# Attention scores listed ahead of older groups' work on TensorE, with six score tiles, eight tiles for maxima and two resident weight pairs fewer

## The chip, the core and the metric

The kernel runs on one core of a Trainium2 chip. The metric is the device time of one execution in microseconds (us). PE is TensorE, PEld its weight load, DVE is VectorE, ACT is ScalarE, POOL is GpSimd, and SP issues the transfers (DMA). Each engine runs its own list of instructions in the order of the program and waits on semaphores for the others.

## What is computed

```python
# q, k, v: 4 batches x 8 heads x 576 x 64, float32, tau = 0.02
scores = scale * q @ k.T
thresh = max(scores, axis=-1) - tau
scores = where(scores >= thresh, scores, -1e9)
attn = exp(scores - max(scores)); attn = attn / (sum(attn) + 1e-9)
x = (attn @ v)                      # as 2304 tokens x 512
h = x @ w_in;  x = (h * sigmoid(1.702 * h)) @ w_out          # d_ff 2048
h = x @ w_in2; out = (h * tanh(softplus(h))) @ w_out2
```

The weights of the two feed-forward layers come as 64-bit floats, and the kernel converts them on the chip.

## The kernel before

**Attention** works on 16 pairs of heads (a "head pair" below), each in five groups: four "full" groups of 128 query rows for both heads, and one "mix" group with the last 64 rows of both. That makes 80 groups, numbered 0 to 79. A group g goes through these steps:

- S(g), scores: `qk` (L600) has PE write the scores of both heads into the PSUM tiles `sc0` and `sc1`. There is one set of them, so S(g+1) must wait until both are read.
- DVE L622 reads a score tile, scales and negates it into an SBUF tile of the ring `ss` (four tiles, two per full group), and puts the negated maximum into a tile of the ring `nm`. POOL L626 adds tau to it.
- ACT L629 takes the exponential into a pair tile of the ring `p` (four, one per group). DVE L632 zeroes what lies below the threshold and sums the rows.
- T(g), transposes: PE L706 and L701 transpose the group's probabilities into `tb0`, `tb1`, `tb2`. ACT L717 copies them into `pm` and `pmt`.
- A(g), attention times v: PE L731 multiplies with `vr` into one half of the PSUM tile `tb3`, the two halves in turn. ACT L738 copies the result into `xo`.

After a head pair's fifth group, the sums are inverted (DVE L648, L649), spread over partitions through DRAM (`r_d`, `rb`), multiplied in (POOL L667) and stored.

**Layer 1** then loops over blocks of tokens and 16 slices f of d_ff: H(f), twelve matmuls into one of four banks `h` (L495), an activation on ACT and DVE (L521 to L527), and O(f), twelve matmuls into `tb0` to `tb3` (L540). PE's order is H0 H1 H2 O0 H3 O1 H4 O2 and so on. Layer 2 has the same shape.

**Weights.** Slice f needs a pair of tiles, `wh` and `wl`, in float32 parts. A chain makes them: a load into one of three `sr` tiles, ACT L380 and L382, DVE L386 and L389, POOL L392, DVE L394, ACT L400 (`wh`), DVE L402 (`wl`). In layer 1 the chain for slice f may start at group 40 + 5f. The first `NWA` pairs have memory from the start. The others lie where attention's tiles were, and wait until attention is over.

**What sets the order.** Nothing runs as it is written. Each piece of work is listed with an engine, a duration, the tiles that it reads and writes, and a rank. A planner (`Order.run`) steps through time: on each engine, of the pieces whose inputs and tiles are free, the one with the lowest rank goes next. The result is a fixed list for each engine. In attention the rank is the group's number, a little less for some steps: scores and transposes of group g have rank g on PE, and A(g) has g - 0.1. DVE's L622 has g - 2.5. The weights have ranks above 5000, so they go into what is left.

Of the kernel before, what the change touches and what calls it, by code (L numbers as in the profile page):

```python
# [11 lines left out]
F32 = mybir.dt.float32  # L12
# [7 lines left out]
SMR = 2.5  # L20
DMA_US = 2.0
DMA_RATE = 200e3
PR = 2
AR = 0.1
NORM_P = 1.0
# [7 lines left out]
SLACK = 0.0  # L33
AHEAD = 2
NP = 8
NSS = 4
NOUT = 2
NHS = 5
NWA = 12
NPM = 4  # L40
NKQ = 2
NXO = 2
# [8 lines left out]
class Order:  # L51
# [23 lines left out]
    def add(self, eng, dur, fn, r=(), w=(), rank=0.0, deps=(), nbytes=None, port=False, steps=1):  # L75
        n = len(self.ops)
        if port:
            self.port.add(n)
        before = set(deps)
        for key in r:  # L80
            if key in self.writer:
                before.add(self.writer[key])
        for key in w:
            if key in self.writer:
                before.add(self.writer[key])
            before.update(self.readers.get(key, ()))
        for key in r:
            self.readers.setdefault(key, []).append(n)
        for key in w:
            self.writer[key] = n  # L90
            self.readers[key] = []
        before.discard(n)
        self.ops.append((eng, dur, fn, before, rank, nbytes, steps))
        return n

    def run(self):
# [19 lines left out]
        while done < n_ops:  # L116
# [34 lines left out]
            if nbytes is not None:  # L151
                wire = end = max(wire, end + DMA_US) + nbytes / DMA_RATE
            order.append((t, i))
# [47 lines left out]
def attention_then_two_ffn_kernel(  # L201
# [46 lines left out]
    apool = att_ctx.enter_context(tc.tile_pool(name="a", bufs=1))  # L248
# [34 lines left out]
    tb = [psum.tile([128, 512], F32, name=f"tb{i}") for i in range(4)]  # L283
# [24 lines left out]
    def t_act(n, ptr=0, psum=True):  # L308
        return (0.05 if psum else 0.09) + n * 0.833e-3 + 0.093 * ptr
# [28 lines left out]
    def make_w(pool, upto):  # L338
        for f in range(len(W), upto):
            W.append([pool.tile([128, 2 * DM], F32R, name=f"w{p}{f}") for p in "hl"])  # L340

    make_w(wpool, NWA)

# [55 lines left out]
    def split_w(f, val, kval, rank):  # L399
        add("ACT", t_act(2 * DM, psum=False), lambda: nc.scalar.copy(W[f][0], val),  # L400
            [kval], [("wh", f)], rank, [opened] if f >= NWA else [])
        add("DVE", t_dve(2 * DM), lambda: nc.vector.tensor_tensor(W[f][1], val, W[f][0], ALU.subtract),  # L402
# [157 lines left out]
    vrs = Ring(apool, "vr", NKQ, [128, 5 * 128], F32)  # L560
    pps = Ring(apool, "p", NP // 2, [128, P1 + S + 1], F32)
    sss = Ring(apool, "ss", NSS, [128, S + 5], F32)
    nms = Ring(apool, "nm", 4, [128, 2], F32)
    sms = Ring(apool, "sm", 2, [128, 32], F32)
    rts = Ring(apool, "rt", 1, [128, 32], F32)
    rbs = Ring(apool, "rb", 1, [128, S], F32)
# [14 lines left out]
    def qk(tl, rank):  # L581

        kind, b, hp, t = tl
        kq2, _, kkq, _ = head[b, hp]
        q0 = S + t * 128

        def mm():
            if kind == "full":
                parts = [(i, sc[i][:, g, 0:SH], g * SH, SH) for g in range(2) for i in range(2)]
            else:  # L590
                lo, hi = sc[0][0:64], sc[0][64:128]
                parts = [
                    (0, lo[:, 0, 0:SH], 0, SH), (1, hi[:, 1, 0:512 - SH], SH + 64, 512 - SH),
                    (1, hi[:, 1, 512 - SH:SH], 0, 64),
                    (0, lo[:, 1, 0:SH], SH, SH), (1, hi[:, 0, 0:SH], 64, SH),
                ]
            for i, dst, k0, n in parts:
                rows = slice(64 * i, 64 * i + 64)
                q = kq2[rows, q0:q0 + (128 if kind == "full" else 64)]
                nc.tensor.matmul(dst, q, kq2[rows, k0:k0 + n], start=True, stop=True)  # L600
                yield

        n = 4 if kind == "full" else 2
        add("PE", n * 0.25 + 0.25, mm, [kkq], [("sc", i) for i in range(n)], rank,
            steps=4 if kind == "full" else 5)
        return [(sc[i][:, :, 0:SH], [("sc", 2 * i), ("sc", 2 * i + 1)]) for i in range(n // 2)]
# [68 lines left out]
    def attend(tl, ps, pair, rank):  # L675

        kind, b, hp, t = tl
        full = kind == "full"
        _, vr, _, kvr = head[b, hp]
        w = 128 if full else 64  # L680
        at = t * 128
        if t == 0:
            xo[b, hp] = xos.next()
        if full:
            plan = [(0, pms, (0, 1), 128, 512), (1, pms, (2, 3), 128, 512), (2, pmt, (4,), 128, 128)]
        else:
            plan = [(0, pms, (0, 1, 2, 3), 128, 512), (1, pmt, (4,), 64, 128)]
        where, copies, keys = {}, [], []
        for bank, ring, cs, rows, cols in plan:
            pn, kpn = ring.next()  # L690
            keys.append(kpn)
            for n, c in enumerate(cs):
                where[c] = (bank, n * 2 * w, pn)
            copies.append((bank, pn, kpn, rows, cols))

        def tr(cs):
            for c in cs:
                bank, c0, _ = where[c]
                if c == 4:
                    m = 64 * len(ps)  # L700
                    nc.tensor.transpose(tb[bank][0:m, 0:128], pair[:, 516:516 + m], ident)  # L701
                    yield
                    continue
                for i in range(len(ps)):
                    a = (P1 + 64 if i else 4) + c * 128
                    nc.tensor.transpose(  # L706
                        tb[bank][:, c0 + i * 128:c0 + (i + 1) * 128], pair[:, a:a + 128], ident)
                    yield

        for (bank, pn, kpn, rows, cols), (*_, cs, _, _) in zip(copies, plan):  # L710
            n = 1 if 4 in cs else len(ps) * len(cs)
            n = add("PE", n * 0.109 + (0.16 if bank == 0 else 0.0), lambda cs=cs: tr(cs),
                ps, [("tb", bank)], rank, steps=max(n, 2))
            if sch.fill is None and WARM:
                sch.fill = ("PE", n, 0.107, keep_warm)
            add("ACT", t_act(cols),
                lambda pn=pn, bank=bank, rows=rows, n=cols: nc.scalar.copy(pn[0:rows, 0:n], tb[bank][0:rows, 0:n]),  # L717
                [("tb", bank)], [kpn], rank)
        i = avn[0] % 2
        avn[0] += 1  # L720
        av, kav = tb[3][:, i * 128:i * 128 + w], ("tb", 3, i)

        def mm():
            for c in range(5):
                _, c0, pn = where[c]
                for i in range(2):
                    rows, at, vc = slice(0, 128), c0 + i * w, c * 128 + 64 * i
                    if c == 4:
                        rows = slice(64 * i, 64 * i + 64) if full else slice(0, 64)
                        at, vc = (0, 512) if full else (64 * i, 512 + 64 * i)  # L730
                    nc.tensor.matmul(  # L731
                        av[64 * i:64 * i + 64], vr[rows, vc:vc + 64], pn[rows, at:at + w],
                        start=(c == 0), stop=(c == 4))
                    yield

        add("PE", len(CK) * 0.107 * (2 if full else 1) + 0.2, mm, keys + [kvr], [kav], rank - AR, steps=2 * len(CK))
        x, kx = xo[b, hp]
        add("ACT", t_act(w), lambda: nc.scalar.copy(x[:, at:at + w], av), [kav], [kx + (t,)], rank - AR)  # L738
        if not full:
            scaling.append(scale_x(b, hp))  # L740

    avn = [0]
# [32 lines left out]
    for gi, tl in enumerate(groups + [None] * AHEAD):  # L775
        first = len(sch.ops)
        if tl:
            for bh in preps.get(gi, []):
                prep(*bh, gi - PR)
            kind, b, hp, t = tl  # L780
            if t == 0:
                sm[b, hp] = sms.next()
            sums, ksum = sm[b, hp]
            pair, kpair = pps.next()
            ps = [softmax_a(sums, ksum, 5 * i + t, gi, bank, (pair, kpair), i)
                  for i, bank in enumerate(qk(tl, gi))]
            marks.append(len(sch.ops) - 1)
            behind.append((tl, ps, pair, gi))
        if gi >= AHEAD:
            attend(*behind.pop(0))  # L790
            for todo in list(scaling):
                todo.pop()(gi - AR, [marks[min(gi, len(marks) - 1)]] if tl else [])
                if not todo:
                    scaling.remove(todo)
        if tl is None and gi == len(groups) + AHEAD - 1:
            for todo in scaling:
                while todo:
                    todo.pop()(gi - AR, [])
        att.extend(range(first, len(sch.ops)))
# [199 lines left out]
```

## Time and profile before

| what | value |
|---|---|
| median of 3 runs | 1096.7 us (1096.17 to 1097.32) |
| the profiled execution | 1097.12 us |
| its span, first to last instruction | 1095.3 us |
| PE busy | 1084.9 us (99%) |
| DVE busy | 692.8 us (63%) |
| ACT busy | 651.2 us (59%) |
| POOL busy | 196.4 us (18%) |
| mean granted clock of PE | 0.998 |

The profiled execution lies 1.8 us over its span and 0.4 us over the median. The busy shares are means over three stages that differ: attention up to about 312 us, layer 1 up to about 698 us, layer 2 to the end. A matmul's end is modelled in this profile, so that a busy PE can still be waiting for a part of its work. The distance from the start of one block of matmuls to the start of the next is the safer measure.

### The profile page before, as it was taken

The numbers are of one execution on the slowest core, as the hardware profiler recorded it, in microseconds if no ns is written. First come the engines' busy times: TensorE is split into PE (matmuls) and PEld (weight loads), VectorE is DVE, ScalarE is ACT, GpSimd is POOL, SyncE is SP. The second block draws the span as 40 slices with busy tenths as digits, with TensorE's granted clock in tenths as the row PEclk, the third lists the DMA queues.
The fourth block names the chain that finished last, engine by engine and source line by source line (L and its number), as shares of the span: only waits on it lengthen the run. The fifth ranks groups of instructions, "written<-read, shape, count | busy, mean of one in ns | idle before, by whom it ended". The sixth has DMA issues, their size and how long they took to land.

```text
span 1095.3 us, 17534 instructions
## 1 busy us (share of the span) xinstructions
PE 1084.9 (99%) x6708; PEld 877.5 (80%) x6708; DVE 692.8 (63%) x1354; ACT 651.2 (59%) x1065; POOL 196.4 (18%) x198
## 2 busy tenths in 40 slices
PE   9999999999999999999999999999999999999998
PEld 7767776777778899888888888888888888888887
DVE  7868899999978645545522444566464555554544
ACT  5767777888856445444422444496655655655665
POOL 2323344455534303303200000000000000000000
PEclk9999999999999999999999999999999999999999
DMA  2223333444244255545510222500010010010010
GB/s 90 82 76 125 92 118 127 146 128 149 95 161 140 94 202 173 199 148 184 181 58 1 97 96 96 173 1 1 29 39 1 10 39 1 1 40 1 1 40 19
DMA packets 49156, 94.53 MB, mean 86 GB/s; under 512 B 6320, under 2 KB 24240, under 8 KB 49072
## 3 DMA queue, kind: packets, MB, share of 16 engines
q1 hardware_dynamic: 49072, 93.42, 25.7%
q8 instruction: 52, 0.85, 0.3%
q14 instruction: 32, 0.26, 0.1%
HBM read 70.78 MB, written 22.62 MB: 85 GB/s over the span
## 4 chain that ended last, share of the span: by engine, by line
PE 97%; ACT 1%; DVE 1%; issue 0%; POOL 0%; POOLq 0%; DVEq 0%; ACTq 0%
PE h L495 36%; PE tb L540 18%; PE tb L911 18%; PE tb L731 9%; PE sc L600 8%; PE tb L706 7%; PE tb L701 1%; PE tb L506 0%; DVE p L632 0%; DVE ss L622 0%; ACT p L629 0%; POOL nm L626 0%; ACT pm L717 0%; ACT xo L738 0%; ACT sv L380 0%
## 5 line engine op out<-in xcount | busy, mean ns | idle before, releaser
L873 ACT ACTIVATE ms<-ms 128x512 f32<-128x512 f32 (+1 forms) x240 | 131.4, 584 | 133.5 <-DVE ms L858 132.5
L495 PE MATMUL h<-xa,wh 128*128 128x512 f32 x640 | 197.5, 390 | 0.0
L495 PE MATMUL h<-x,wh 128*128 128x512 f32 (+1 forms) x640 | 165.2, 346 | 0.0
L495 PEld LDWEIGHTS h<-xa,wh 128*128 128x128 f32 x640 | 119.7, 188 | 24.7 <-issue 0.2
L521 ACT ACTIVATE t<-h 128x512 f32<-128x512 f32 (+1 forms) x80 | 44.5, 557 | 155.3 <-PE h L495 154.7
L632 DVE SCALAR_TENSOR_TENSOR p<-ss,nm,p 128x577 f32<-128x577 f32 x144 | 130.0, 926 | 8.1 <-ACT p L629 6.4
L629 ACT ACTIVATE p<-ss,nm 128x576 f32<-128x576 f32 x144 | 111.5, 785 | 37.9 <-DVE ss L622 37.4
L524 DVE SCALAR_TENSOR_TENSOR h<-t,h 128x512 f32<-128x512 f32 (+1 forms) x80 | 51.3, 642 | 121.4 <-ACT t L521 121.2
L883 DVE TENSOR_TENSOR ms<-ms,hs 128x512 f32<-128x512 f32 (+1 forms) x80 | 50.2, 636 | 122.3 <-ACT ms L873 122.2
L622 DVE TENSOR_SCALAR_CACHE_REDUCE ss<-sc,nqsc 128x576 f32<-128x576 f32 x144 | 112.2, 812 | 21.1 <-PE sc L600 20.4
L495 PEld LDWEIGHTS h<-x,wh 128*128 128x128 f32 x640 | 112.7, 189 | 15.8
L495 PE MATMUL h<-xa,wl 128*128 128x512 f32 x320 | 124.5, 389 | 0.0
L626 POOL TENSOR_SCALAR nm<-nm,tau_p 128x1 f32<-128x1 f32 x144 | 88.0, 612 | 168.0 <-DVE ss L622 163.6
L540 PE MATMUL tb<-gh,wh 128*128 128x512 f32 (+1 forms) x320 | 117.8, 368 | 0.0
L540 PE MATMUL tb<-gl,wh 128*128 128x512 f32 (+1 forms) x320 | 117.7, 368 | 0.0
L540 PE MATMUL tb<-gh,wl 128*128 128x512 f32 (+1 forms) x320 | 117.7, 368 | 0.0
L392 POOL TENSOR_TENSOR sv<-sv,sr 128x1024 uint32<-128x1024 uint32 x32 | 83.4, 2608 | 175.7 <-DVE sv L389 104.8
L911 PE MATMUL tb<-wh,g2h 128*128 128x512 f32 x288 | 112.1, 389 | 0.0
L911 PE MATMUL tb<-wl,g2h 128*128 128x512 f32 x288 | 112.1, 389 | 0.0
L911 PE MATMUL tb<-wh,g2l 128*128 128x512 f32 x288 | 112.0, 389 | 0.0
L495 PE MATMUL h<-x,wl 128*128 128x512 f32 (+1 forms) x320 | 110.9, 347 | 0.0
L600 PE MATMUL sc<-kq 64*128 64x288 f32 (+3 forms) x672 | 105.0, 417 | 1.0 <-DVE ss L622 0.9
(59 smaller groups left out, 1756.0 us busy)
## 6 DMA issues: line engine op xcount, KB each, us to landing
sr<-in_w_in SPq DMA_DIRECT2D x32, 512.0 KB
sr<-in_w_out SPq DMA_DIRECT2D x32, 512.0 KB
kq<-in_kq SPq DMA_DIRECT2D x16, 576.0 KB
sv<-x_d SPq DMA_DIRECT2D x16, 512.0 KB
w_d<-sv SPq DMA_DIRECT2D x16, 512.0 KB
sv<-w_d SPq DMA_DIRECT2D x16, 512.0 KB
vr<-in_v SPq DMA_DIRECT2D x16, 320.0 KB
x_d<-xo SPq DMA_DIRECT2D x16, 288.0 KB
```

Of the source, the lines that this page charges most:

```text
L392: lambda: nc.gpsimd.tensor_tensor(bits, bits, word(0), ALU.add), keys, [kval], rank, port=True)
L495: nc.tensor.matmul(hb[dst][:, 0:n], a[:, c, :], x[:, lo, c, 0:n], start=(i == 0), stop=(i == 3 * KD - 1))
L540: nc.tensor.matmul(accs[e][0][:, 0:n], a[:, es], b()[:, 0:n], start=(f == 0 and i == 0), stop=(f == KF - 1 and i == 2), skip_group_check=True,
L600: nc.tensor.matmul(dst, q, kq2[rows, k0:k0 + n], start=True, stop=True)
L622: lambda: nc.vector.tensor_scalar(n3, s3, nqsc, None, ALU.mult, ALU.min, accum_out=nm[:, 0:1]),
L626: lambda: nc.gpsimd.tensor_scalar(nm[:, 1:2], nm[:, 0:1], tau_p, 0.0, ALU.add, ALU.add),
L629: lambda: nc.scalar.activation(p[:, at:at + S], ns[:, 4:4 + S], AF.Exp, bias=nm[:, 0:1], scale=-1.0),
L632: lambda: nc.vector.scalar_tensor_tensor(p[:, whole], ns[:, 3 + i:4 + S + i], nm[:, 1:2], p[:, whole], ALU.is_le, ALU.mult, accum_out=sums ...
L706: nc.tensor.transpose(tb[bank][:, c0 + i * 128:c0 + (i + 1) * 128], pair[:, a:a + 128], ident)
L731: nc.tensor.matmul(av[64 * i:64 * i + 64], vr[rows, vc:vc + 64], pn[rows, at:at + w], start=(c == 0), stop=(c == 4))
L873: nc.scalar.activation(m()[:, 0:n], m()[:, 0:n], fn, bias=bias)
L911: nc.tensor.matmul(accs[t][0], x[:, t * 128:(t + 1) * 128], w, start=(f == 0 and i == 0), stop=(f == KF - 1 and i == 2), skip_group_check= ...
```

## The change

Five things are edited. The scores' rank on PE becomes g - 8 instead of g, so that among ready work on PE the scores of a group come before transposes and products of groups up to seven older. The ring `ss` has six tiles instead of four, and `nm` eight instead of four. The product of a mix group goes into the unused half of `tb2` instead of a half of `tb3`. `NWA` falls from 12 to 10, so weight pairs 10 and 11 now wait for the end of attention too.

```diff
+SF = 8
...
-NSS = 4
+NSS = 6
...
-NWA = 12
+NWA = 10
...
-    nms = Ring(apool, "nm", 4, [128, 2], F32)
+    nms = Ring(apool, "nm", 8, [128, 2], F32)
...
-        i = avn[0] % 2
-        avn[0] += 1
-        av, kav = tb[3][:, i * 128:i * 128 + w], ("tb", 3, i)
+        if full:
+            i = avn[0] % 2
+            avn[0] += 1
+            av, kav = tb[3][:, i * 128:i * 128 + w], ("tb", 3, i)
+        else:
+            av, kav = tb[2][:, 256:256 + w], ("tb", 2, 1)
...
-                  for i, bank in enumerate(qk(tl, gi))]
+                  for i, bank in enumerate(qk(tl, gi - SF))]
```

Line numbers after the edits are one to four higher than before. The planner's lists show what moves. In its rows a name ends in a tile's number within the program; `p0` to `p3` are the pair tiles of groups 4n to 4n+3.

First place: PE around group 14, the mix group of the third head pair. Before, from T(14) on (L706 and L701 are transposes, L731 products, L600 scores):

```order
L706 MATMUL tb0_91<-ident_100,p2_158 128x128 x4
L701 MATMUL tb1_92<-ident_100,p2_158 64x128
L731 MATMUL tb3_94<-pm0_172,vr0_154 64x128 x4
L731 MATMUL tb3_94<-pm1_173,vr0_154 64x128 x4
L731 MATMUL tb3_94<-pmt1_177,vr0_154 64x128 x2
L731 MATMUL tb3_94<-pm2_174,vr0_154 64x64 x8
L731 MATMUL tb3_94<-pmt0_176,vr0_154 64x64 x2
L600 MATMUL sc0_98<-kq1_153 128x288
L600 MATMUL sc1_99<-kq1_153 128x288
L600 MATMUL sc0_98<-kq1_153 128x288
L600 MATMUL sc1_99<-kq1_153 128x288
```

These are T(14), A(13), A(14) and then S(15): no score stood between S(14) and S(15) while the transposes of groups 12 to 14 and the products A(11) to A(14) went by. Now, from A(13) on:

```order
L735 MATMUL tb3_94<-pm0_174,vr0_150 64x128 x4
L735 MATMUL tb3_94<-pm1_175,vr0_150 64x128 x4
L735 MATMUL tb3_94<-pmt1_179,vr0_150 64x128 x2
L702 MATMUL tb1_92<-ident_100,p2_154 64x128
L707 MATMUL tb0_91<-ident_100,p3_155 128x128 x4
L601 MATMUL sc0_98<-kq1_149 128x288
L601 MATMUL sc1_99<-kq1_149 128x288
L601 MATMUL sc0_98<-kq1_149 128x288
L601 MATMUL sc1_99<-kq1_149 128x288
L735 MATMUL tb2_93<-pm2_176,vr0_150 64x64 x8
L735 MATMUL tb2_93<-pmt0_178,vr0_150 64x64 x2
L707 MATMUL tb1_92<-ident_100,p3_155 128x128 x4
```

Here S(18) stands between A(13) and A(14), and A(14) writes `tb2`. Over the whole list, the last scores ahead of a product A(g) are now S(g+5) in 46 of the 75 cases up to H0 and S(g+4) in 18; before they were S(g+3) in 65 of 77. Changes from one kind of work to another, from S(0) to O0, fall from 252 to 243, since the transposes stand in 84 blocks instead of 93.

Second place: PE from the last score matmuls, S(79), to the first of layer 1, H0. Before:

```order
L600 MATMUL sc0_98<-kq1_153 64x288 x2
L706 MATMUL tb0_91<-ident_100,p1_157 128x128 x4
L731 MATMUL tb3_94<-pm1_173,vr1_155 64x128 x4
L731 MATMUL tb3_94<-pm2_174,vr1_155 64x128 x4
L731 MATMUL tb3_94<-pmt0_176,vr1_155 64x128 x2
L706 MATMUL tb1_92<-ident_100,p1_157 128x128 x4
L701 MATMUL tb2_93<-ident_100,p1_157 128x128
L706 MATMUL tb0_91<-ident_100,p2_158 128x128 x4
L495 MATMUL h0_3113<-xa_151,wh0_116 128x512 x2
```

Now:

```order
L601 MATMUL sc0_98<-kq1_149 64x288 x2
L707 MATMUL tb0_91<-ident_100,p2_154 128x128 x4
L702 MATMUL tb1_92<-ident_100,p2_154 64x128
L702 MATMUL tb2_93<-ident_100,p3_155 128x128
L707 MATMUL tb0_91<-ident_100,p3_155 128x128 x4
L735 MATMUL tb2_93<-pm2_176,vr0_150 64x64 x8
L735 MATMUL tb2_93<-pmt0_178,vr0_150 64x64 x2
L707 MATMUL tb1_92<-ident_100,p3_155 128x128 x4
L707 MATMUL tb0_91<-ident_100,p0_152 128x128 x4
L702 MATMUL tb2_93<-ident_100,p0_152 128x128
L496 MATMUL h0_3061<-xa_147,wh0_116 128x512 x2
```

H0 moves ahead by two groups' work: before, A(77) to A(79) and the transposes T(78) in part and T(79) stand behind H0; now A(75) to A(79) and T(76) in part to T(79) do. Before O0 stand, in both, all of attention and H0, H1, H2. The last pieces before O0 are, before, A(78) H2 T(79) A(79), and now H2 A(77) T(78) T(79) A(78) T(79) A(79).

Third place: DVE from the last L622, that of group 79, on (L402 makes `wl`, L394 the step of the weights' chain ahead of `wh`, L524 and L527 belong to layer 1). Before:

```order
L622 TENSOR_SCALAR ss3_163,nm3_167<-sc0_98,nqsc_103 128x576
L632 SCALAR_TENSOR_TENSOR p2_158,sm1_169<-ss2_162,nm2_166,p2_158 128x577
L402 TENSOR_TENSOR wl4_125<-sv0_113,wh4_124 128x1024
L394 SCALAR_TENSOR_TENSOR sv1_114<-sr2_112,sv1_114 128x1024
L386 TENSOR_SCALAR sv2_115<-sv2_115 128x1024
L386 TENSOR_SCALAR sv0_113<-sv0_113 128x1024
L389 TENSOR_SCALAR sv2_115<-sv2_115 128x1024
L402 TENSOR_TENSOR wl5_127<-sv1_114,wh5_126 128x1024
L389 TENSOR_SCALAR sv0_113<-sv0_113 128x1024
L524 SCALAR_TENSOR_TENSOR h0_3113<-t0_143,h0_3113 128x512
```

Now:

```order
L623 TENSOR_SCALAR ss5_161,nm7_169<-sc0_98,nqsc_103 128x576
L633 SCALAR_TENSOR_TENSOR p1_153,sm1_171<-ss1_157,nm3_165,p1_153 128x577
L633 SCALAR_TENSOR_TENSOR p1_153,sm1_171<-ss2_158,nm4_166,p1_153 128x577
L633 SCALAR_TENSOR_TENSOR p2_154,sm1_171<-ss3_159,nm5_167,p2_154 128x577
L633 SCALAR_TENSOR_TENSOR p2_154,sm1_171<-ss4_160,nm6_168,p2_154 128x577
L395 SCALAR_TENSOR_TENSOR sv2_115<-sr0_110,sv2_115 128x1024
L395 SCALAR_TENSOR_TENSOR sv0_113<-sr1_111,sv0_113 128x1024
L390 TENSOR_SCALAR sv1_114<-sv1_114 128x1024
L525 SCALAR_TENSOR_TENSOR h0_3061<-t0_139,h0_3061 128x512
L528 TENSOR_TENSOR gl0_144<-h0_3061,gh0_141 128x512
L633 SCALAR_TENSOR_TENSOR p3_155,sm1_171<-ss5_161,nm7_169,p3_155 128x577
```

Before layer 1's first L524, six weight pairs were finished (`wl0` to `wl5`); now three are (`wl0` to `wl2`), and `wl3`, `wl4`, `wl5` follow behind the L524 of slices 1 and 2. The last threshold step of attention (L632 of group 79) stood behind L527 of slice 1 and now stands behind that of slice 0. From `wl8` on, both lists put the pairs at about the same place among layer 1's steps.

## Rows read from the trace of the kernel before

**Rows 1.** Timeline of PE, attention at full pace: start us, us, instruction, [idle before].

```profile
284.17 0.66 PE L706 MATMUL tb<-ident,p 128*128 128x128 f32 x4
...
284.87 1.24 PE L600 MATMUL sc<-kq 64*128 64x288 f32 x8
286.44 0.69 PE L731 MATMUL tb<-pm,vr 128*64 128x64 f32 x16 [0.33 <-ACT pm L717]
...
287.32 1.09 PE L706 MATMUL tb<-ident,p 128*128 128x128 f32 x8
...
288.45 1.24 PE L600 MATMUL sc<-kq 64*128 64x288 f32 x8
289.62 1.09 PE L731 MATMUL tb<-pm,vr 128*64 128x128 f32 x16
...
291.01 1.09 PE L706 MATMUL tb<-ident,p 128*128 128x128 f32 x8
...
292.15 1.20 PE L600 MATMUL sc<-kq 64*64 64x288 f32 x10
293.27 0.65 PE L706 MATMUL tb<-ident,p 128*128 128x128 f32 x4
```

**Rows 2.** Timeline of PE: the first scores, and the first O block.

```profile
5.80 1.24 PE L600 MATMUL sc<-kq 64*128 64x288 f32 x8
...
311.87 0.50 PE L540 MATMUL tb<-gh,wh 128*128 128x512 f32 x1
```

**Rows 3.** Groups of PE, 12 to 312 us: count, busy, mean ns, idle before, its releasers.

```profile
L600 PE MATMUL sc<-kq 64*128 64x288 f32 (+3 forms) x655 | 102.2, 417 | 1.0 <-DVE ss L622 0.9
L706 PE MATMUL tb<-ident,p 128*128 128x128 f32 x568 | 83.5, 282 | 1.5 <-DVE p L632 1.5
L731 PE MATMUL tb<-pm,vr 128*64 128x128 f32 (+1 forms) x1280 | 82.0, 269 | 2.7 <-ACT pm L717 1.4 <-ACT xo L738 1.1
```

**Rows 4.** Timeline of PE and one row of DVE, where scores came late.

```profile
63.30 0.82 DVE L622 TENSOR_SCALAR_CACHE_REDUCE ss<-sc,nqsc 128x576 f32<-128x576 f32 x1 [5.63 <-PE sc L600]
...
64.18 1.97 PE L600 MATMUL sc<-kq 64*128 64x288 f32 x8 [0.91 <-DVE ss L622]
...
66.85 1.51 PE L706 MATMUL tb<-ident,p 128*128 128x128 f32 x7 [0.44 <-DVE p L632]
```

**Rows 5.** Windows: stretch, us, busy of PE, PEld, DVE, ACT, POOL, granted clock, DMA.

```profile
66.00:68.00 2.00, 1.56 (x9) 1.29 (x9) 2.00 (x5) 0.43 (x1) 0.29 (x1) 0.79 0.00 0
68.00:70.00 2.00, 2.00 (x9) 1.35 (x9) 1.10 (x4) 2.00 (x5) 0.90 (x1) 0.50 0.01 4
...
175.00:300.00 125.00, 124.30 (x1248) 89.35 (x1248) 121.74 (x280) 105.75 (x210) 63.75 (x74) 1.00 0.41 132
300.00:375.00 75.00, 73.18 (x362) 59.63 (x359) 61.83 (x71) 44.88 (x63) 32.40 (x11) 1.00 0.41 137
```

**Rows 6.** Timeline of PE at attention's last two blocks.

```profile
309.14 0.66 PE L706 MATMUL tb<-ident,p 128*128 128x128 f32 x4 [0.73 <-DVE p L632]
...
310.99 0.69 PE L731 MATMUL tb<-pm,vr 128*64 128x64 f32 x16 [1.09 <-ACT pm L717]
```

**Rows 7.** Timeline of DVE and PE: the weight pairs 14 and 15, and H(14) and H(15).

```profile
370.54 1.22 DVE L402 TENSOR_TENSOR wl<-sv,wh 128x1024 fp32r<-128x1024 f32 x1
...
374.01 1.23 DVE L402 TENSOR_TENSOR wl<-sv,wh 128x1024 fp32r<-128x1024 f32 x1 [0.51 <-ACT wh L400]
...
374.56 0.62 PE L495 MATMUL h<-xa,wh 128*128 128x512 f32 x2
...
380.00 0.62 PE L495 MATMUL h<-xa,wh 128*128 128x512 f32 x2
```

**Rows 8.** Line L394 of DVE, one per weight pair, 290 to 376 us: ns min/median/max, first and last start.

```profile
L394 DVE SCALAR_TENSOR_TENSOR sv<-sr,sv x11: 1162/1214/1226, 296.2 to 371.7; 128x1024 uint32<-128x1024 uint32 x11
```

**Rows 9.** Timeline of SP: the last store of attention's result.

```profile
330.25 0.33 SPq L669 DMA_DIRECT2D x_d<-xo  x1
```

## Prediction

> **What bounds the kernel now.** First the table: PE is busy 99% of the span, at full clock but for a dip. From O0 on it runs twelve matmuls every 2.72 us (H(14) and the O block behind it take 5.44 us, [rows 7]) and is without idle time, so layers 1 and 2 hold no time to win; they can only lose, if a weight pair comes late. What the change can win lies between the first scores at 5.80 and O0 at 311.87, 306.07 us [rows 2].
>
> How much of that is work? In the timeline of PE at full pace, start to start, a full group takes 1.17 for S (288.45 to 289.62), 1.39 for A (to 291.01) and 1.14 for T (to 292.15): 3.70 us. A mix group takes 1.12 (292.15 to 293.27), 0.88 (286.44 to 287.32) and 0.70 (284.17 to 284.87): 2.70 [rows 1]. So 64 x 3.70 + 16 x 2.70 = 280.0; H0 to H2 add 8.2, and sixteen warm-up transposes between S(0) and S(1) about 2.0 (an estimate at 1.14 / 9 each). That is 290.2, and 15.9 us are something else:
>
> - Idle PE: 1.0 + 1.5 + 2.7 = 5.2 by what ended it [rows 3]. It sits in two bad places and some small ones. At 64 to 67 us PE waits 0.91 and 0.44 [rows 4]: the list had let products and transposes of four groups go ahead of S(15), DVE had stood 5.63 us without a score, and PE then waited for DVE to catch up. At 309 to 312 us it waits 0.73 and 1.09 for attention's last group [rows 6]. That is 1.35 + 1.82 = 3.17 in the two, 2.0 elsewhere.
> - The clock: behind the first bad place the mean grant is 0.79 and then 0.50 over two stretches of 2 us, that is, PE fell to the lower of its two levels, 1.2 GHz, for a part of them, right after the waits at 64 to 67 us [rows 4, 5]. Lost: 0.21 x 2 + 0.50 x 2 = 1.4.
> - Split transposes: 9 in one block take 1.14, 5 take 0.70, so one costs 0.11 and a block's end 0.15. They stand in 93 blocks where 80 would do: 13 x 0.15 = 2.0.
> - The rest, 7.3, is hidden in blocks that look busy. An example is S at 284.87, which takes 1.57 instead of 1.17 [rows 1], as when its second tile is still being read by DVE.
>
> **The change, part by part.**
>
> *Scores first.* No instruction of PE is added. The bad place at 64 us goes: in the new list S(15) to S(18) stand ahead of A(14), DVE has scores to work on, and its 1.35 us go, with the dip behind it, 1.4. Nothing like the stretch without a score is left in the list. The last group's chain goes too: S(79) is now followed by the work of groups 74 to 78 and H0 to H2 before T(79), and the last L632 stands behind L527 of slice 0 instead of slice 1 (third place in the list). That is 1.82. Elsewhere I take the new list to be as tight as the old one outside its bad places, 2.0 idle and 7.3 hidden, neither better nor worse; the bounds are none of the 7.3 left, and as much again. Nine blocks of transposes fewer give 9 x 0.15 = 1.4 (1.35).
>
> *More tiles for scaled scores and maxima.* They let L622 go three groups ahead of L632 instead of two; without them the lead of S could not grow. They cost four one-column clears on DVE before the first score, which PE's warm-up covers.
>
> *Products of mix groups in `tb2`.* Idle time that ends with ACT's copy of `xo` is 1.1 us in all [rows 3]. I count none of it, because the halves of `tb3` still alternate for full groups; all of it is the upper bound.
>
> *Two weight pairs without memory of their own, and all pairs later.* Here a loss can come from. At layer 1's first L524, three pairs are ready instead of six. Today pair 14 is finished at 370.54 + 1.22 = 371.76 for H(14) at 374.56, and pair 15 at 375.24 for H(15) at 380.00: a slack of 2.8 and 4.8 us [rows 7]. Pairs come 7.55 us apart there ((371.7 - 296.2) / 10, [rows 8]), but slices are needed every 5.44, so the chain as it runs now loses ground. What hides the added work is DVE's idle time: from 300 to 375 us it is busy 61.83 of 75, 13.2 free [rows 5]. Three more pairs need about 3 x 3.8 = 11.4 (two steps of 1.22 each, two that I take at 0.7). It just fits. Also, H0 starts about two groups' T and A, 2 x 2.53 = 5.1 us, earlier in PE's list, and DVE steps of the chain that stand behind L524 follow it. Pairs 10 and 11 wait for attention's last store, issued at 330.25, 18.4 us behind O0 [rows 9]; H(10) starts 2.72 + 7 x 5.44 = 40.8 us behind O0, so that wait costs nothing unless `wh` is made more than 20 us ahead. I take no stall. The bounds are 0 and one pair behind, 7.55 - 2.8 = 4.8.
>
> Sum: 3.17 + 1.42 + 1.35 = 5.9 us. The profiled execution of 1097.1 becomes 1091.2, and since it lay 0.4 over the median, I say 1090.8, a gain of 0.54%. About 0.2%, or 2.2 us, is what a measurement of this kernel can tell from no change.
>
> **The rivals.**
>
> *The weights cap the gain.* If the pairs come at the times of today, H(14) cannot start before 371.8 and H(15) not before 375.2, whatever attention gains: the gain is 2.8 to 4.8 us, so 1091.9 to 1093.9. For it: the chain is slower than its use [rows 8]. Against: its steps on DVE stand behind layer 1's, which come earlier.
>
> *The weights come late: slower.* Place: PE waits at H(12) to H(15). If they are d us later than today, the whole is d - 2.8 slower; from d = 5.0 on it is slower by 0.2%. One pair's distance, 7.55, gives 4.8 us: 1101.5. For it: three pairs fewer at the start, and DVE would have to be busy 73.2 of 75. Against: part of DVE's idle time was waiting for layer 1.
>
> *Scores just in time.* A score that is listed the moment its tiles should come free blocks PE if DVE is late, with ready transposes queued behind it. The row for it is the S that took 0.40 too long [rows 1]. If fifteen more scores of the 80 are held so, 6.0 us are gone and the result is today's, about 1096.5; from twenty it is slower than today by 2.1. For it: in 175 to 300 us DVE is busy 121.74 of 125 [rows 5]. Against: DVE has three pairs' work, 11.4 us, less in attention. The Trainium skill (TensorE: Matmul & The Clock Gate, The mechanism) speaks for it: matmuls start and end strictly in program order, and only weight loads are pulled ahead. The trace agrees: at 66.85 and 309.14 PE stood still with other matmuls queued [rows 4, 6]. By that rule alone every late score is paid in full.
>
> *The lead does nothing.* The ring `p` still has four pair tiles, so exponentials of group g wait for T(g-4). If DVE is the bound from 175 us on, scores ahead only wait longer, and the repaired tail alone is left: 1.8 us, 1094.9, no change that can be told.
>
> **How the numbers follow.** Forecast (gain of 4.5 us or more) 0.52; capped by the weights 0.14; just in time 0.16; no effect 0.07; late weights 0.11. Faster: 0.52 + 0.12 of the cap's 0.14 = 0.64. Same: 0.02 of the cap, 0.12 of just in time, 0.07 = 0.21. Slower: 0.11 + 0.04 = 0.15. For the range: if half of the 7.3 hidden and all 1.1 of `xo` go too, it is 4.7 lower, 1086.1; I start at 1086.5. Above, it takes in the cap, no change, and late weights up to d = 5.1: 1099.0.
>
> **What would show it.** The step on scores is right if the timeline of PE has no idle time over 0.4 us before H0, a clock of 1.00 from 50 to 75 us, and O0 at about 306. The step on weights is right if PE has no idle time from O0 to H(16), with pair 15 finished before H(15). The forecast is wrong if PE's idle time before scores, or S blocks longer than 1.17, add up to more than now, or if H(12) to H(15) wait for L402.

## The result, and the profile after

| | before | after |
|---|---|---|
| median | 1096.97 us (1096.17 to 1097.32, 4 runs) | 1088.44 us (1088.21 to 1088.53, 4 runs) |
| profiled execution | 1097.12 us | 1088.53 us |
| its span | 1095.3 us | 1086.8 us |
| S(0) to O0 | 306.07 us | 297.55 us |

The ratio is 0.9918 (0.9906 to 0.9931): 8.5 us, or 0.8%, faster. O0 comes at 303.33 instead of 311.87. From there to the end both kernels take 783.4 us, so the whole gain lies before O0, in attention.

First, the groups of PE from 12 to 304 us (count, busy, mean ns, idle before, its releasers), to be held against [rows 3].

```profile
L601 PE MATMUL sc<-kq 64*128 64x288 f32 (+3 forms) x655 | 98.8, 413 | 1.0 <-DVE ss L623 1.0
L707 PE MATMUL tb<-ident,p 128*128 128x128 f32 x568 | 82.1, 278 | 1.6 <-ACT pm L718 1.6
L735 PE MATMUL tb<-pm,vr 128*64 128x128 f32 (+1 forms) x1280 | 81.0, 269 | 0.0
L735 PE MATMUL tb<-pmt,vr 64*64 64x128 f32 (+1 forms) x320 | 33.2, 284 | 0.4 <-ACT pmt L718 0.4
L702 PE MATMUL tb<-ident,p 128*128 128x128 f32 (+1 forms) x79 | 22.7, 290 | 0.2 <-ACT pm L718 0.2
```

Idle time fell from 5.2 to 3.2 us. Its kind changed too: the waits for `xo` and for L632 (L633 now) are gone, and 2.2 us of waits for the copies into `pm` and `pmt` are there.

Where the first bad place was [rows 4], PE's timeline now has a score between any two products, at the pace of [rows 1]: 1.17 from S to A, 61.04 to 62.21.

```profile
61.04 1.24 PE L601 MATMUL sc<-kq 64*128 64x288 f32 x8
62.21 1.09 PE L735 MATMUL tb<-pm,vr 128*64 128x128 f32 x16
...
64.27 1.24 PE L601 MATMUL sc<-kq 64*128 64x288 f32 x8
65.44 0.69 PE L735 MATMUL tb<-pm,vr 128*64 128x64 f32 x16
...
67.01 1.20 PE L601 MATMUL sc<-kq 64*64 64x288 f32 x10
```

The windows (columns as in [rows 5]) show the full clock there. In 300 to 375 us PE has 1.4 us more work than before in the same stretch, with DVE as busy as before.

```profile
66.00:70.00 4.00, 4.00 (x49) 2.81 (x43) 3.60 (x11) 3.37 (x7) 1.74 (x3) 1.00 0.46 120
70.00:75.00 5.00, 4.81 (x48) 3.42 (x46) 4.16 (x11) 3.32 (x9) 2.00 (x3) 1.00 0.40 147
175.00:300.00 125.00, 123.44 (x1244) 90.59 (x1239) 118.69 (x270) 101.41 (x206) 55.45 (x67) 1.00 0.40 125
300.00:375.00 75.00, 74.60 (x362) 61.45 (x360) 61.87 (x67) 46.24 (x62) 31.95 (x11) 1.00 0.43 141
```

The end of attention on PE, where 0.73 and 1.09 stood [rows 6], has one wait of 0.40.

```profile
301.99 0.69 PE L735 MATMUL tb<-pm,vr 128*64 128x64 f32 x16
303.07 0.33 PE L735 MATMUL tb<-pmt,vr 64*64 64x64 f32 x4 [0.40 <-ACT pmt L718]
303.33 0.50 PE L541 MATMUL tb<-gh,wh 128*128 128x512 f32 x1
```

The weight pairs 14 and 15 on DVE, and H(14) and H(15) on PE, as in [rows 7]: pair 15 is ready at 371.21 for an H(15) at 371.47. The slack of 4.8 us has become 0.3 (the first matmul that reads that `wl` starts at 371.93), and PE still does not wait.

```profile
361.71 1.22 DVE L403 TENSOR_TENSOR wl<-sv,wh 128x1024 fp32r<-128x1024 f32 x1
...
366.03 0.62 PE L496 MATMUL h<-xa,wh 128*128 128x512 f32 x2
...
369.98 1.23 DVE L403 TENSOR_TENSOR wl<-sv,wh 128x1024 fp32r<-128x1024 f32 x1 [1.12 <-ACT wh L401]
...
371.47 0.62 PE L496 MATMUL h<-xa,wh 128*128 128x512 f32 x2
```

**Where the 8.5 us came from.** Take PE's timeline from S(0) to O0, block by block, from one start to the next, and subtract from each block the idle time that the trace shows in it:

| | before | after | difference |
|---|---|---|---|
| S blocks | 99.6 | 96.0 | -3.6 |
| T blocks | 86.4 | 85.2 | -1.3 |
| A blocks | 104.1 | 102.4 | -1.6 |
| H blocks and warm-up | 10.8 | 10.7 | -0.1 |
| idle | 5.2 | 3.25 | -2.0 |
| sum | 306.1 | 297.55 | -8.5 |

The clock sits in the first two rows. Experiment 3 gives its share: there both bad places are still as they were, idle is 5.18, but the clock did not fall in that execution, and the S and T blocks are 0.8 and 0.6 us shorter: 1.4 together. Its A blocks are 0.5 shorter for another reason. Two products in a row, of a full and a mix group, took 2.59 and 2.49 net of idle in the kernel before (at 59.08 and 119.38) and take 2.27 with `tb2`. Experiment 4, which lacks `tb2` and has the full clock at both places, still shows 2.59 and 2.49. So this 0.5 is the work of `tb2`, not of the clock. Net of the clock, 2.8 (S), 0.65 (T) and 1.6 (A) went: 5.1 us that looked like busy PE.

On DVE, the waits of L622 for scores before 300 us fell from 17.1 us to 5.8. First before, then after (total, times, longest):

```profile
DVE ss L622 <- PE sc L600: 17.1, 23, 5.6
```

```profile
DVE ss L623 <- PE sc L601: 5.8, 16, 0.7
```

### The profile page after: what moved, and what is told of

It is laid out like the page before. It is cut to its first block, busy times and chain, and to the rows that moved or that the text cites. A ratio compares the mean times of both kernels' runs of the same rounds, so it can differ in the third digit from the quotient of the medians.

```text
span 1086.8 us, 17469 instructions
## 1 busy us (share of the span) xinstructions
PE 1078.3 (99%) x6708; PEld 873.7 (80%) x6708; DVE 690.9 (64%) x1358; ACT 651.3 (60%) x1065; POOL 184.0 (17%) x198
## 4 chain that ended last, share of the span: by engine, by line
PE 98%; ACT 1%; DVE 1%; issue 0%; POOL 0%; ACTq 0%; DVEq 0%; POOLq 0%
PE h L496 36%; PE tb L541 18%; PE tb L915 18%; PE tb L735 9%; PE sc L601 8%; PE tb L707 6%; PE tb L702 1%; ACT pm L718 1%; DVE p L633 0%; PE tb L507 0%; DVE ss L623 0%; ACT p L630 0%; DVE o L927 0%; DVE sv L387 0%; ACT gh L527 0%
## 5 line engine op out<-in xcount | busy, mean ns | idle before, releaser
L633 DVE SCALAR_TENSOR_TENSOR p<-ss,nm,p 128x577 f32<-128x577 f32 x144 | 130.8, 932 | 15.7 <-ACT p L630 8.3
L623 DVE TENSOR_SCALAR_CACHE_REDUCE ss<-sc,nqsc 128x576 f32<-128x576 f32 x144 | 112.2, 812 | 9.7 <-PE sc L601 9.0
L627 POOL TENSOR_SCALAR nm<-nm,tau_p 128x1 f32<-128x1 f32 x144 | 75.1, 522 | 167.5 <-DVE ss L623 165.1
```

Source lines behind the costliest of these rows:

```text
L623: lambda: nc.vector.tensor_scalar(n3, s3, nqsc, None, ALU.mult, ALU.min, accum_out=nm[:, 0:1]),
L627: lambda: nc.gpsimd.tensor_scalar(nm[:, 1:2], nm[:, 0:1], tau_p, 0.0, ALU.add, ALU.add),
L633: lambda: nc.vector.scalar_tensor_tensor(p[:, whole], ns[:, 3 + i:4 + S + i], nm[:, 1:2], p[:, whole], ALU.is_le, ALU.mult, accum_out=sums ...
```

## The experiments

The theory: the new order of scores is the whole gain, since it leaves no stretch in which DVE has no score; the tiles, `tb2` and `NWA` only allow it. Rivals: the extra tiles, or `tb2`, win time by themselves; fewer resident pairs cost some of it; scores that are merely earlier anywhere are enough. Unless another base is named, an edit is made to the kernel before, and the ratio is to before, with its 95% interval.

**1. All tiles, `tb2` and `NWA`, scores back at rank g** (base: after).

```diff
-SF = 8
+SF = 0
```

> The changed kernel with the scores' rank back at g (SF = 0): six score tiles, eight tiles for maxima, ten resident pairs and the product in tb2 stay. In its list the lead of S over A is 3 again in 58 of 76 cases, and four products still pass without a score around group 14. Theory 'the order is it': the place at 64 us comes back with its clock dip, the tail may be mended, so 1094 to 1096.5. Rival 'the tiles are it': the room for scaled scores carries the gain, and it stays at 1088 to 1090.

1095.26 us, ratio 0.9987 (0.9978 to 0.9996). O0 is at 310.82, and the waits of 0.91 and 0.5 us at 63 to 66 us are back. Without the rank the other edits are worth 0.1%.

**2. The rank and `tb2` alone**: four `ss`, four `nm`, twelve pairs.

```diff
-        i = avn[0] % 2
-        avn[0] += 1
-        av, kav = tb[3][:, i * 128:i * 128 + w], ("tb", 3, i)
+        if full:
+            i = avn[0] % 2
+            avn[0] += 1
+            av, kav = tb[3][:, i * 128:i * 128 + w], ("tb", 3, i)
+        else:
+            av, kav = tb[2][:, 256:256 + w], ("tb", 2, 1)
...
-                  for i, bank in enumerate(qk(tl, gi))]
+                  for i, bank in enumerate(qk(tl, gi - 8))]
```

> The kernel before with the rank g - 8 and the product in tb2 alone: four score tiles, four tiles for maxima, twelve resident pairs. The lead of S over A is 4 or 5 in 65 cases, 84 blocks of transposes, five pairs ready at H0 instead of three. Theory 'the order is it': O0 at 303 to 305 us, 1088.5 to 1090.5. Rival 'the tiles are it': scores wait for L622, L622 waits for a free score tile, S blocks stretch to more than before, 1093 to 1097.

1088.16 us (1087.53 to 1088.52), ratio 0.9919 (0.9905 to 0.9932): all of the gain. O0 is at 302.74. Pair 14 is ready 1.0 us before H(14), and pair 15 2.4 us before H(15) (368.37 and 370.74). So the extra tiles add nothing that can be measured, and with twelve pairs the slack is small too. The lead did grow with four tiles: the last score ahead of A(g) is S(g+4) or S(g+5) in 65 of 76 cases. The rank with the mix product left in `tb3` wasn't tried, since two products would then write one bank side by side without an order between them; that `tb2` makes the rank possible is all that is claimed for it.

**3. `tb2` alone** (the first hunk of experiment 2).

> The kernel before with the product of mix groups in tb2 and nothing else; the list is that of before. The idle time of PE that ends with the copy to xo was 1.1 us. If it was that half of tb3, PE's idle time there goes and the time falls by 0.5 to 1.1 us, to 1095.8 to 1096.4; by the prediction, which counted nothing, 1096.9.

1096.78 us, ratio 0.9996 (0.9987 to 1.0005): nothing that the ratio can tell. In the trace, two of the three waits for `xo` give way to waits of 0.34 us for `pmt`, and the A blocks lose the 0.5 us named above. The profiled execution kept its clock behind the same gaps: in its window the grant is 1.00, where a mean of 0.79 and 0.50 stood [rows 5].

```profile
66.00:70.00 4.00, 3.96 (x36) 2.90 (x36) 3.83 (x11) 3.24 (x6) 1.49 (x3) 1.00 0.01 2
```

**4. Two resident pairs fewer, alone.**

```diff
-NWA = 12
+NWA = 10
```

> The kernel before with ten resident weight pairs instead of twelve; the list up to H0 is that of before. Theory 'no cost': wh of slice 10 was written at 340 us, 10 us behind the last store of attention, so nothing waits: 1096.5 to 1097.3. Rival 'late pairs': the two pairs wait for attention's memory, the chain behind them is late, and H(12) to H(15) wait: 1098.5 to 1102.

1097.49 us, ratio 1.0003 (0.9994 to 1.0012), every pair with its slack of before or up to 1.5 us more. No cost.

**5, 6 and 7. The rank in one part of the program**: `tb2`, and g - 8 for groups 0 to 23, 24 to 69, or 70 to 79.

```diff
+                  for i, bank in enumerate(qk(tl, gi - (8 if gi < 24 else 0)))]
```

> The kernel before with the product in tb2 and the rank g - 8 for groups 0 to 23 alone. In its list the stretch around group 14 without a score is gone, the tail is nearly as before. By the prediction's terms: 0.91 + 0.44 of idle time and up to 1.4 of clock, 1.4 to 2.8 us, so 1094.3 to 1095.8. Rival 'only the lead everywhere counts': within 0.5 us of before.

> The kernel before with the product in tb2 and the rank g - 8 for groups 24 to 69 alone. The bad place at 64 us stays. By the prediction, which took the hidden 7.3 us and the small idle times as unchanged, only the tail changes (T(79) two blocks later): 1095 to 1097. Rival 'the hidden waits in S blocks go too': S blocks sum to about 97 us instead of 100.8 before O0, and the time falls by 3 to 5 us, to 1092 to 1094.

> The kernel before with the product in tb2 and the rank g - 8 for groups 70 to 79 alone. By the prediction the tail's 0.73 + 1.09 = 1.8 us go: 1095.2. Rival 'the tail only moves': the last chain waits elsewhere, 1096.5 to 1097.

Groups 0 to 23: 1094.56 us, ratio 0.9979 (0.9970 to 0.9988). The bad place at 64 us is gone. The two waits at the end of attention are gone as well, though no rank was changed there: the planner's list shifts behind an edit too. But the waits of 64 us, the same to the hundredth of a microsecond, stand further on in PE's timeline:

```profile
151.68 1.97 PE L600 MATMUL sc<-kq 64*128 64x288 f32 x8 [0.91 <-DVE ss L622]
...
154.35 0.98 PE L706 MATMUL tb<-ident,p 128*128 128x128 f32 x7 [0.44 <-DVE p L632]
```

Groups 24 to 69: 1098.35 us, ratio 1.0010 (1.0001 to 1.0019). In that trace the place at 64 us is as before, and three scores further on wait 0.76, 0.92 and 1.24 us for L622. Groups 70 to 79: 1101.63 us, ratio 1.0041 (1.0028 to 1.0053), slower. This is the rival "scores just in time", and the forecast of a gain for experiment 7 fell. In its trace the end of attention has one wait of 1.59 us instead of two of 1.8 in sum. PE's waits from 255 to 300 us are four for L622, and one of 0.2 us for `pm`; the S blocks are 2.6 us longer than in experiment 3, net of idle. In 265 to 283 us DVE is busy without a break while PE is not:

```profile
PE sc L600 <- DVE ss L622: 2.4, 4, 0.7
```

```profile
265.00:283.00 18.00, 15.83 (x145) 10.48 (x141) 18.00 (x42) 14.19 (x28) 12.95 (x12) 1.00 0.36 112
```

Each time, the products and transposes listed behind the score stood too. The Trainium skill (TensorE: Matmul & The Clock Gate, The mechanism) says that matmuls start and end in program order; these four waits agree with it. Scores early in one part only are therefore not enough.

**8 and 10. A lead of three.** Experiment 8 is after with SF = 3. Experiment 10 is before with `tb2` and g - 3, so with four `ss`, four `nm`, twelve pairs.

```diff
-                  for i, bank in enumerate(qk(tl, gi))]
+                  for i, bank in enumerate(qk(tl, gi - 3))]
```

> The changed kernel with SF = 3 instead of 8. In its list the lead of S over A is 3 in 71 of 76 cases, as before the change, but no more than two products pass between scores; transposes stand in 108 blocks instead of 84; six pairs are ready at H0. If a block's end costs 0.15 us, as the prediction says, 24 more blocks cost 3.6 us and the time is about 1092. Rival 'the block ends are free', since the transposes now wait for copies anyway: 1088 to 1089.5. Rival 'the lead of five groups is needed': scores wait as before, 1094 or more.

> The kernel before with the product in tb2 and the rank g - 3: four score tiles, twelve pairs, a lead of 3 in 73 of 77 cases, 109 blocks of transposes, six pairs at H0. Theory 'an even order is it, the lead and the tiles are not': 1089 to 1091, with pair 15 ready 8 us or more ahead of H(15). Rival 'the even order needs the six tiles': scores wait, 1093 or more.

1090.12 us, ratio 0.9939 (0.9926 to 0.9951), and 1089.29 us, ratio 0.9934 (0.9921 to 0.9946). In both lists the last score ahead of a product is S(g+3) almost throughout, as before the change. So 7 to 8 of the 8.5 us need no longer lead. What differs from before is the order: at most two products stand between two scores, where four did at S(15). That count is not all of it, since the list of experiment 9 below keeps to it too and gains less. From the start of one group's score to the next, the longest stretch on PE is 9.8 us before, 6.3 in experiment 9, and 4.8 in experiments 8 and 10; in the changed kernel it is 4.9. The two waits at the end of attention are one of 0.62 in experiment 8 and none in experiment 10. The waits of PE in experiment 10, 12 to 310 us, are down to one:

```profile
PE sc L600 <- DVE ss L622: 0.2, 1, 0.2
```

These lists split the transposes into 108 and 109 blocks instead of 84. T then takes 88.05 us net of idle instead of 85.15 in both, 2.9 for 24 or 25 blocks: 0.12 each.

**9. Only the stretch without scores mended**: `tb2` and g - 1. The list is nearly that of before, its lead and the two waits at its end too (0.71 and 1.11 us here), but no more than two products stand between scores.

```diff
-                  for i, bank in enumerate(qk(tl, gi))]
+                  for i, bank in enumerate(qk(tl, gi - 1))]
```

> The kernel before with the product in tb2 and the rank g - 1. Its list is nearly that of before: a lead of 3 in 65 of 77 cases, 94 blocks of transposes, the same tail, six pairs at H0, but no more than two products pass between scores. Theory 'the stretch without scores is a cause of its own': DVE's 5 us wait for scores at 63 us goes, with the 1.35 us behind it and the dip, so 1094 to 1095.5, and the tail's 1.8 us stay. Rival 'order matters only through the lead': 1096 to 1097.5.

1093.61 us, ratio 0.9972 (0.9961 to 0.9984), 3.2 us under experiment 3. But its six executions fall into two groups by the granted clock: three at 1.00 take 1092.6 to 1092.7 us, three at 0.998 take 1094.5 to 1094.8. Like against like, it is 2.3 to 2.4 us under experiment 3 (1094.98 at 1.00, a median of 1096.97 at 0.998). So the stretch is a cause of its own, of that size, and the clock still falls in half of the executions without it.

**11. The weights' chain started later** (base: after).

```diff
-C0 = 40
+C0 = 60
```

> The changed kernel with the weights' chain of slice f allowed from group 60 + 5f instead of 40 + 5f; two pairs instead of three are ready at H0. Theory 'the weights cap the gain': pair 15 is ready 0.3 us ahead of H(15) in the changed kernel, so one pair fewer at H0 (a pair is 7 us of its chain) shows as idle time of PE that ends with L403 among H(3) to H(15), 3 to 10 us, and the time is 1091 to 1098. Rival 'the chain has room': DVE and ACT have idle time enough to catch up, no idle time of PE, 1088 to 1089.

1092.94 us, ratio 0.9966 (0.9953 to 0.9979), 4.5 us over after. Attention is even shorter, O0 at 302.22, but layer 1 now waits for weights. PE, then DVE (one period of the chain):

```profile
359.81 0.50 PE L496 MATMUL h<-xa,wl 128*128 128x512 f32 x1 [0.53 <-DVE wl L403]
...
366.14 0.50 PE L496 MATMUL h<-xa,wl 128*128 128x512 f32 x1 [0.53 <-DVE wl L403]
```

```profile
358.53 1.22 DVE L403 TENSOR_TENSOR wl<-sv,wh 128x1024 fp32r<-128x1024 f32 x1
359.67 0.68 DVE L528 TENSOR_TENSOR gl<-h,gh 128x512 fp32r<-128x512 f32 x1
360.27 2.33 DVE L387 TENSOR_SCALAR sv<-sv 128x1024 f32<-128x1024 f32 x1
362.52 1.21 DVE L395 SCALAR_TENSOR_TENSOR sv<-sr,sv 128x1024 uint32<-128x1024 uint32 x1
363.66 0.68 DVE L525 SCALAR_TENSOR_TENSOR h<-t,h 128x512 f32<-128x512 f32 x1
364.26 0.68 DVE L390 TENSOR_SCALAR sv<-sv 128x1024 uint32<-128x1024 uint32 x1
364.86 1.22 DVE L403 TENSOR_TENSOR wl<-sv,wh 128x1024 fp32r<-128x1024 f32 x1
```

DVE has no gap, and a pair comes every 6.33 us (358.53 to 364.86) where PE could use one every 5.44. Not all of that is work: L387 takes 2.33 here and 0.69 in the median, and ends 0.55 behind a step of POOL that takes 358.74 to 362.05 (the last section says more). L395 needs the result of that POOL step, so no run shows how much shorter the period could be. The rival "the weights cap the gain" is a real limit, and with 0.3 us of slack the changed kernel stands right before it.

**12. Experiment 7 without weights in its way**: the same rank, and the chain only from group 78 on.

```diff
-C0 = 40
+C0 = 78
```

> The run with the rank g - 8 for groups 70 to 79 alone, and the weights' chain allowed only from group 78 on. Layer 1 then waits long for its weights, so the whole time says nothing (1130 or more); what counts is PE before H0. Theory 'DVE, loaded with weight pairs, makes the early scores late': the four waits of S for L622 at 266 to 286 us, 2.4 us in all, are gone. Rival 'the sudden lead does it': they stay, 1.5 us or more.

One execution, 1127.51 us, since layer 1 then waits for weights (PE is idle for 12.9 us from O0 on). Only attention is read. PE's waits from 255 to 300 us, and the window of experiment 7:

```profile
PE tb L706 <- ACT pm L717: 0.6, 3, 0.2
```

```profile
265.00:283.00 18.00, 17.82 (x183) 12.98 (x183) 16.55 (x41) 12.99 (x30) 7.48 (x13) 1.00 0.22 70
```

No score waits for L622 any more. So the four waits of experiment 7 hang on the weights' chain. Its steps on DVE (L386, L389, L394, L402) are busy 13.1 us in 255 to 300 us there, and not at all here. The edit also takes away the chain's steps on ACT and POOL, and the planner makes another list without them, so which of these made the scores late is not separated; that it was DVE's load is argued. Nor does a run show why the rank in every group escapes such waits with the chain in place. Before group 70, where both keep rank g, the waits of 0.91 and 0.44 us appear here at 64, 192 and 248 us although no weight step runs. Those are a matter of the list alone.

## Why the prediction was nearly right

The direction, the place and the mechanism of the bad places were right, and the time lies in the range; but the range, 1086.5 to 1099.0, held no change at all as well. The gain was taken too small: 5.9 us against 8.6 in the profiled execution. That it came so near is in part luck. The three terms of the sum, 5.9, measure 4.0 (2.0 idle, 1.4 clock, 0.65 transposes), and 4.4 came from two terms that were put at nothing (2.8 in S blocks, 1.6 in A blocks). Of the signs named, the clock is 1.00 from 50 to 75 us and PE does not wait in layer 1, but there are three idle times over 0.4 us before H0 (0.48, 0.86 and 0.51).

- **Scores first, the bad place.** 1.35 + 1.42 were summed. Between two profiled executions at full clock (O0 - S(0) of 304.06 in experiment 3 and 301.69 in 9) the mended stretch is worth 2.4, of which 1.4 idle, as summed, and 0.9 inside S blocks. The clock's 1.4 was right for the profiled execution, but it is not there in all: of the 59 timed executions of the kernel before beside the experiments, 14 show a mean granted clock of 1.0 and take 1095.4 to 1095.6 us, 43 show 0.998 and take 1096.7 to 1098.0, and two show 0.995 and take 1099.5. Between the first two groups lie some 1.9 us. Of after, all four show 1.0; at equal clock the gain is 7.0 us. Nor does the fall belong to this place alone: see experiment 9 above and the last section.
- **The tail.** 1.82 became 0.40, as the step said but for that rest.
- **"As tight as the old one outside its bad places, 2.0 idle and 7.3 hidden".** This step failed, in both directions. Idle ended at 3.25, not 2.0: 2.2 us of new waits for L718 and 1.0 for two late scores. The hidden part was mis-sized by more: S blocks lost 2.8 us net of the clock. An S that has waited for its first tile then waits for the second inside its block: it takes 1.97 at 64.18 [rows 4], and 1.97 again at 276.35 in after, where 1.24 is usual, so 0.73 belongs to each such wait and is not in the idle column. In the bad place alone two S blocks are 0.8 and 0.45 too long (experiment 3, at full clock). From 100 to 300 us nine blocks were 0.2 to 0.7 too long, 3.6 in all; after, five, 2.8 in all. These were listed as a bound (half of the 7.3) and should have been in the sum. The example given for them was wrong: of the 1.57 from the S at 284.87 to the A behind it, 0.33 is the idle time in A's own row [rows 1], which was already in the 5.2. And 0.7 of the 7.3 was no wait: H0 to H2 take 8.9 net of idle, not 8.2, in both kernels.
- **Products.** A lost 1.6 us, where nothing was counted. Of these, 0.5 is what `tb2` gives (experiment 3). Another 0.4 is one block of 1.82 us at 165.63, with a wait for `xo` in its middle, where 1.39 is usual; experiment 3 still has it, after does not. Most of the rest is in five blocks of after that stand ahead of a mix group's score and take 1.29; why these are shorter is open.
- **Nine blocks of transposes fewer.** The price of 0.15 was near (0.12 measured), and T is 0.65 us shorter net of idle and clock, against 1.35. But longer blocks brought the waits for L718: four of 0.18 or 0.19 us in blocks of 10 and 13 transposes, and 0.48 and 0.51. Experiment 8, with 24 blocks more, has 1.58 us of idle time in all, and experiment 10, with 25 more, takes only 0.8 us longer from S(0) to O0 (298.34). So this term is worth little in the end.
- **Tiles.** "Without them the lead of S could not grow" was wrong: experiment 2 has a lead of four and five with four tiles.
- **Weights.** No stall, as taken. But it fits by 0.3 us. The load was looked for in the wrong place: DVE is no busier from 300 to 375 us (61.87 against 61.83), since by 300 us five pairs are ready in both kernels. The slack went because H(15) comes 8.5 us earlier and pair 15 only 4.0. One rival was 0.3 us away, and experiment 11 shows its price.
- **Just in time.** Right as a mechanism (experiments 6 and 7), not for this change: with the lead from the first group on, two late scores of 0.86 and 0.17 us are left. (Fifteen late scores would have given 1096.8 by that rival's own sum, not 1096.5.)

## What to carry to other kernels

Look in the list of the bounding engine for the longest stretch in which it feeds nothing to the engine behind it, and even that out before buying deeper rings: here one number in a rank, with the place of one product moved to allow it, was the whole gain, and two tiles, four maxima and two weight pairs bought nothing. A "busy" block that takes longer than the same block elsewhere is a wait, and shrinks with its cause. Work that is moved ahead of ready work pays only while the engine that frees its tiles is not late, so look at what else that engine does there.

## What was not expected of the hardware

**DVE stands while POOL works on SBUF.** The late score of after, and the longest of experiment 6, follow a DVE step that took three to four times its usual time (0.82 for L633, 0.69 for L386). After: DVE, then POOL, then PE.

```profile
272.04 2.90 DVE L633 SCALAR_TENSOR_TENSOR p<-ss,nm,p 128x577 f32<-128x577 f32 x1 [0.23 <-POOL nm L627]
...
277.89 0.82 DVE L623 TENSOR_SCALAR_CACHE_REDUCE ss<-sc,nqsc 128x576 f32<-128x576 f32 x1
...
271.92 2.40 POOL L393 TENSOR_TENSOR sv<-sv,sr 128x1024 uint32<-128x1024 uint32 x1
...
277.88 2.39 POOL L393 TENSOR_TENSOR sv<-sv,sr 128x1024 uint32<-128x1024 uint32 x1
...
276.35 1.97 PE L601 MATMUL sc<-kq 64*128 64x288 f32 x8 [0.86 <-DVE ss L623]
```

Experiment 6, in the same order:

```profile
246.04 2.88 DVE L386 TENSOR_SCALAR sv<-sv 128x1024 f32<-128x1024 f32 x1
...
245.49 2.88 POOL L392 TENSOR_TENSOR sv<-sv,sr 128x1024 uint32<-128x1024 uint32 x1
...
249.71 2.60 PE L600 MATMUL sc<-kq 64*128 64x288 f32 x8 [1.24 <-DVE ss L622]
```

DVE's step ends 0.62 us after POOL's (274.94 and 274.32), and 0.55 in experiment 6 (248.92 and 248.37), however long it has stood: the same last part of its work is left when POOL ends. This is the rule here: before 390 us, all 22 DVE steps over 1.3 us in the kernel before, and all 22 in after, start while such a POOL step (L667 or L392, one line later in after) runs, and end 0.55 to 0.62 or 1.08 to 1.09 us behind it. The trace counts the standing as busy time: 8.7 of DVE's 121.74 us in 175 to 300 us [rows 5] are such. L623, which reads PSUM, starts with a POOL step at 277.88 and takes its usual 0.82. The Trainium skill (SBUF — State Buffer, SBUF: two separate sides) says that DVE and GpSimd share a pair of ports under an exclusive lock, held for a whole instruction; the rows agree. No run here moved these steps apart, so that the late score would vanish then is argued, not shown.

**The clock falls in some executions only, and not always in the same place.** With the same waits in both bad places (the kernel before, experiments 3 and 4, within 0.02 us), PE was at the lower of its two levels, 1.2 GHz, for a part of 66 to 70 us in the first execution (a mean of 0.79 and 0.50, [rows 5]) and at the full 2.4 GHz there in the other two. In experiment 4 it fell behind the last waits of attention instead:

```profile
308.00:312.00 4.00, 2.89 (x28) 2.21 (x29) 4.00 (x7) 2.71 (x6) 0.00 (x0) 0.80 0.21 52
312.00:316.00 4.00, 4.00 (x16) 3.20 (x15) 2.65 (x3) 1.86 (x2) 0.00 (x0) 0.78 0.86 294
```

So a fall can follow either bad place. Experiment 9 mends only the first, and three of its six executions show 0.998; where it fell in those is not on record. With both mended, all four executions of after and all five of experiment 10 show 1.0. In experiment 6, the grant behind the wait of 1.24 us is 0.59 and 0.72 over ten microseconds:

```profile
250.00:255.00 5.00, 5.00 (x35) 3.04 (x34) 4.27 (x12) 2.91 (x8) 1.85 (x4) 0.59 0.10 35
255.00:260.00 5.00, 5.00 (x41) 3.42 (x41) 2.81 (x7) 2.86 (x6) 0.72 (x1) 0.72 0.48 153
```
